# Attention and MLP on one core: native float32 for two units instead of one and a half, the weight decode's word in PSUM, raw weights loaded into their own place

## The chip, the cores and the metric

The kernel runs on one core of a Trainium2 chip. The metric is device microseconds of one execution. The kernel before takes 771.88 us, the median of 3 runs (769.47 to 772.12). The engines are called PE (TensorE), DVE (VectorE), ACT (ScalarE), POOL (GpSimd) and SP (the queue that issues most DMAs).

## The reference

Attention with 4 sink keys and a window of 128, then a two-layer MLP over the 3072 tokens:

```python
# q, k, v: 4 batches, 8 heads, 768 positions, 64 wide; float32
scores = (1 / np.sqrt(64)) * np.matmul(q, k.transpose(0, 1, 3, 2))
keep = is_sink | ((rel >= 0) & (rel < window))        # rel = query position - key position
scores = np.where(keep, scores, -1000000000.0)
scores = scores - np.max(scores, axis=-1, keepdims=True)
a = np.exp(scores)
a = a / (np.sum(a, axis=-1, keepdims=True) + 1e-09)
x = heads_side_by_side(np.matmul(a, v))               # 3072 x 512
h = x @ w_in                                          # 512 x 2048
out = np.maximum(0.01 * h, h) @ w_out                 # 2048 x 512
```

The weights arrive as 64-bit floats and are turned into float32 words on the chip by shifts and masks.

## The kernel before

**Units.** The work is cut into 8 units (`NU`): a batch has two, each with 384 query positions (`TU`), that is `T` = 3 tiles of 128. Tile `s1_3_2` holds the scores of unit 1, head 3, query tile 2. In the first unit of a batch the first query tile sees one block of 128 keys; every other tile sees two blocks, with the 4 sinks between them: 260 columns (`W3`).

**Attention of a head.** `load_head` brings queries and keys, transposed and written twice into 128 rows, `load_next` is called one head ahead. `scores` multiplies; `softmax` on a 260-column tile first writes the previous block's columns over those of the own block that lie in the future (`copy_predicated` with the mask `tri`, the *select*), so that 128 + 4 columns are left, then scales, masks and takes the maximum in one DVE instruction, exponentiates on ACT, and normalises. `tail` transposes on PE, ACT copies the result out of PSUM, and `place` (two affine selects on POOL) separates the two key blocks again. `sinks` gathers the sink columns of a pair of heads, `values` multiplies by v, `emit_x` splits the result into a rounded high part and a rest (`xh`, `xl`).

**Two precisions.** *Native* takes float32 operands as they are, in one product; each is two PE instructions in the profile. *Split* has a high and a low part as `fp32r`, rounded on ACT, the rest by subtraction on POOL or DVE (`split_head`, `split_values`), and two products. `NATH = 9`: the scores of unit 0 and of unit 1's head 0 are native; `NATP = 8`: the values of units 0 and 1 are. All else is split. The MLP is split too, with three products each: `h` in 16 chunks (`fc`) of 12 products, then `o` of 9 products a chunk, which follows one chunk later. `g` is the larger of h and 0.01 h, `gh` and `gl` its parts.

**Weights.** `load_weights(fc)` fetches a raw tile of each matrix (512 KB) into the shared ring `wraw` of two buffers, joins the words on DVE in three steps (L161, L163, L165; the last two read the raw tile and the word, both in SBUF), rounds on ACT (`hi`) and subtracts on POOL (`lo`, L170). `check_weights` later uses the same ring.

**Order.** PE's order is written out by hand: `attention_stream` yields after each tile, and tails, sinks and values stand in the list `pend` until there is credit (`RATE`, `CAP`, `LAG`). Unit 0's attention runs alone, with two chunks decoded meanwhile (`PRE`); then `mlp_stream` takes over and the attention of the next unit is woven in by a due time for each MLP step. Unit 0's MLP also calls `load_weights`, two chunks ahead (`AHEAD`). All other engines' orders come from a scheduler, within the dependences.

**PSUM** has 8 banks: three for o (`ps_o`; during unit 0's attention they hold scores), one each for h (`ps_h`), scores and values, and two for transposes (`ps_t`). Spare matmuls on zeros (`warm`) follow each transpose of unit 0.

Of the kernel before, what the change touches and what calls it, by code (L numbers as in the profile page):

```python
# [117 lines left out]
def fast_path(ctx, tc, cpool, qk, vu, vs, w_in, w_out, out, ident, lim, masks, tri, diag, negm, wmin, wmax):  # L118
# [19 lines left out]

    xs = [[] for _ in range(NU)]
# [5 lines left out]
    def raw_words(nm, fc, name):  # L145
        raw = iopool.tile([P, 512, 2], I32, tag="wraw", name=name, bufs=2)
        if nm == "i":
            src = w_in.rearrange("(c p) f -> p c f", p=P)[:, :, 2 * fc * P:2 * (fc + 1) * P]
            nc.sync.dma_start(out=raw.rearrange("p (c f) t -> p c (f t)", c=NCC), in_=src)
        else:  # L150
            nc.sync.dma_start(out=raw.rearrange("p f t -> p (f t)"), in_=w_out[fc * P:(fc + 1) * P, :])
        return raw

    def load_weights(fc):
        for nm in ("i", "o"):
            raw = raw_words(nm, fc, f"w{nm}raw{fc}")
            top, low = raw[:, :, 1], raw[:, :, 0]
            w = iopool.tile([P, 512], F32, tag="io", name=f"w{nm}{fc}")
            wi = w.bitcast(I32)
            with tc.issue_after(anchor[0].ins):  # L160
                nc.vector.tensor_scalar(out=wi, in0=top, scalar1=3, scalar2=0x3FFFFFFF,  # L161
                                        op0=ALU.logical_shift_left, op1=ALU.bitwise_and)
            nc.vector.scalar_tensor_tensor(out=wi, in0=top, scalar=-0x40000000, in1=wi,  # L163
                                           op0=ALU.bitwise_and, op1=ALU.bitwise_or)
            nc.vector.scalar_tensor_tensor(out=wi, in0=low, scalar=29, in1=wi,  # L165
                                           op0=ALU.logical_shift_right, op1=ALU.bitwise_or)
            hi = wpool.tile([P, 512], F32R, name=f"w{nm}h{fc}")
            lo = wpool.tile([P, 512], F32R, name=f"w{nm}l{fc}")
# [4 lines left out]
    def check_weights(nm, fc):  # L173
        raw = raw_words(nm, fc, f"c{nm}raw{fc}")
# [10 lines left out]
    def native_scores(u, h):  # L185
        return u * H + h < NATH

    def native_values(u, h):
        return NATP0 <= (u * H + h) // 2 < NATP

    def load_head(u, h):
        b, half = divmod(u, 2)
        if native_scores(u, h):
            rows = slice(0, P)
            raw = apool.tile([P, TU + NK[half]], F32, tag="qksp", name=f"qkn{u}_{h}")
        else:
            rows = slice(0, P)
            raw = apool.tile([P, TU + NK[half]], F32, tag="qkraw", name=f"qkraw{u}_{h}", bufs=1)
        nc.sync.dma_start(out=raw[rows, :], in_=qk[half][b, h, rows])
        raws[u, h] = raw  # L200
        if h % 2 == 0:
            if native_values(u, h):
                if h % 4:
                    vr = apool.tile([P, 4 * P], F32, tag="vsp", name=f"vn{u}_{h}", bufs=1)
                else:
                    vr = iopool.tile([P, 4 * P], F32, tag="vraw", name=f"vn{u}_{h}", bufs=1)
                eng = nc.scalar if u + h else nc.sync
            else:
# [40 lines left out]
    wz = wpool.tile([P, TU], mybir.dt.bfloat16, name="wz")  # L249
    nc.gpsimd.memset(wz, 0.0)  # L250

    def keep_warm(u, n):
        if u == 0:
            for _ in range(n):
                nc.tensor.matmul(warm[:, 0:TU], lhsT=wz[:, 0:P], rhs=wz, start=True, stop=True)

    def scores(u, h, j, parts, rows, sp):
# [6 lines left out]
        for c, off in enumerate(parts):  # L264
            nc.tensor.matmul(ps[:, 0:kn], lhsT=sp[rows, off + j * P:off + (j + 1) * P],  # L265
                             rhs=sp[rows, TU + k0:TU + k0 + kn], start=c == 0, stop=c == len(parts) - 1)
        keep_warm(u, WARM)
        return ps

    def softmax(u, h, j, ps, w):  # L270
# [3 lines left out]
        else:  # L274
# [6 lines left out]
                                                   scale=-SCALE * (0.5 if native_scores(u, h) else 1.0), scalar=3.0e38, op0=ALU.add, op1=ALU.min,  # L281
# [19 lines left out]
    slots = [0]  # L301

    def slot():
        slots[0] += 1
        return ps_t.tile([P, P], F32, tag="t", name=f"t{slots[0]}")

    def tail(u, h, j, pk, pt, sk):
# [13 lines left out]
        nc.scalar.copy(out=hi, in_=tp[:, 0:P])
# [396 lines left out]
```

## Time and profile before

| what | value |
|---|---|
| median of 3 runs | 771.88 us (769.47 to 772.12) |
| the profiled execution | 770.29 us, its span 768.5 us |
| mean granted PE clock | 0.984 |
| PE busy | 730.7 us, 95% of the span |
| DVE busy | 586.5 us, 76% |
| ACT busy | 415.3 us, 54% |
| POOL busy | 408.1 us, 53% |
| DMA | 76.73 MB, 100 GB/s in the mean |

Busy time of PE counts a matmul from its start to its modelled end, and matmuls overlap; so two starts in a row tell what one costs in a stream, and the busy share only where PE stands still. Times are counted from the span's start. The span covers 768.5 us of the execution's 770.29.

### The profile page before, as it was taken

How to read it: one execution, taken by the hardware profiler on the slowest of the kernel's cores; microseconds unless marked ns; L12 is line 12 of the kernel's file. 1: busy time of each engine (PE TensorE's matmuls, PEld its weight loads, DVE VectorE, ACT ScalarE, POOL GpSimd, SP SyncE). 2: the span in 40 equal slices, each digit the busy share in tenths (PEclk: the TensorE clock that was granted, in tenths of full speed). 3: DMA queues.
4: the chain of work that ended last, by engine and by line, in shares of the span. 5: the costliest groups of instructions: out<-in, count | busy, mean ns of one | idle time of the engine just before them, and what ended most of it. 6: DMA issues, size and time to landing. Idle time of an engine off the chain costs nothing.

```text
span 768.5 us, 12615 instructions
## 1 busy us (share of the span) xinstructions
PE 730.7 (95%) x3849; PEld 623.9 (81%) x3849; DVE 586.5 (76%) x1884; ACT 415.3 (54%) x1185; POOL 408.1 (53%) x557
## 2 busy tenths in 40 slices
PE   5887898899999999999999999999999999999996
PEld 3445667668888988888888888888898888889895
DVE  7679998997666888888888888888888977733322
ACT  3356555557666566656656566666656555432221
POOL 4237777865455576755665586755665555200000
PEclk8899999999999999999999999999999999999998
DMA  6435555553111243233423442233431321001001
GB/s 237 133 95 174 176 163 169 155 168 123 54 39 63 96 142 101 91 110 115 132 88 96 133 142 95 88 108 123 125 94 63 106 65 40 1 1 42 1 1 46
DMA packets 41707, 76.73 MB, mean 100 GB/s; under 512 B 3616, under 2 KB 24352, under 8 KB 41632
## 3 DMA queue, kind: packets, MB, share of 16 engines
q1 hardware_dynamic: 39920, 73.84, 30.3%
q10 hardware_dynamic: 1712, 2.00, 0.9%
q8 instruction: 33, 0.54, 0.3%
q14 instruction: 42, 0.34, 0.1%
HBM read 69.54 MB, written 6.29 MB: 99 GB/s over the span
## 4 chain that ended last, share of the span: by engine, by line
PE 82%; DVE 11%; DMA 3%; issue 1%; POOL 1%; ACT 0%; DVEq 0%; POOLq 0%; ACTq 0%
PE o L484 33%; PE h L463 32%; PE v L376 9%; PE s L265 5%; PE t L310 2%; DMA woraw<-in_w_out 2%; DVE wo L163 1%; DVE wi L163 1%; DVE wo L161 1%; DVE wi L165 1%; DVE pk L289 1%; DVE pk L280 1%; DVE s L272 1%; DVE wo L165 1%; DVE wi L161 1%
## 5 line engine op out<-in xcount | busy, mean ns | idle before, releaser
L298 POOL TENSOR_SCALAR_AFFINE_SELECT pt<-stg 128x256 fp32r<-128x256 f32 (+1 forms) x320 | 135.5, 448 | 117.8 <-DVE stg L323 50.5
L463 PE MATMUL h<-xh,wih 128*128 128x384 f32 x512 | 189.1, 369 | 5.7 <-DVE g L471 4.6
L463 PE MATMUL h<-xh,wil 128*128 128x384 f32 x512 | 173.6, 339 | 0.8 <-POOL wil L170 0.8
L463 PE MATMUL h<-xl,wih 128*128 128x384 f32 x512 | 173.5, 339 | 0.8 <-DVE xl L426 0.8
L484 PE MATMUL o<-woh,gh 128*128 128x512 f32 x384 | 160.2, 417 | 0.0
L484 PE MATMUL o<-woh,gl 128*128 128x512 f32 x384 | 152.3, 397 | 0.6 <-DVE gl L473 0.5
L484 PE MATMUL o<-wol,gh 128*128 128x512 f32 x384 | 151.6, 395 | 0.0
L471 DVE TENSOR_TENSOR g<-h,g 128x384 f32<-128x384 f32 x128 | 71.0, 554 | 63.7 <-ACT g L470 62.0
L473 DVE TENSOR_TENSOR gl<-g,gh 128x384 fp32r<-128x384 f32 x128 | 103.9, 812 | 17.2 <-ACT gh L472 15.6
L283 ACT ACTIVATE pk<-pk,negm 128x132 f32<-128x132 f32 (+1 forms) x192 | 77.3, 403 | 73.4 <-DVE negm L280 66.4
L463 PEld LDWEIGHTS h<-xh,wih 128*128 128x128 f32 x512 | 96.8, 189 | 23.4 <-DVE g L471 6.0
L226 POOL TENSOR_TENSOR qksp<-qkraw,qksp 64x524 fp32r<-64x524 f32 (+1 forms) x55 | 68.3, 1242 | 74.4 <-issue 54.1
L470 ACT ACTIVATE g<-h 128x384 f32<-128x384 f32 x128 | 62.3, 487 | 72.6 <-PE h L463 72.3
L463 PEld LDWEIGHTS h<-xl,wih 128*128 128x128 f32 x512 | 97.3, 190 | 4.2 <-DVE xl L426 1.1
L463 PEld LDWEIGHTS h<-xh,wil 128*128 128x128 f32 x512 | 96.5, 189 | 1.4 <-POOL wil L170 1.4
L484 PEld LDWEIGHTS o<-woh,gh 128*128 128x128 f32 x384 | 72.4, 188 | 19.1 <-issue 5.5
L484 PEld LDWEIGHTS o<-woh,gl 128*128 128x128 f32 x384 | 72.5, 189 | 18.9 <-DVE gl L473 2.1
L472 ACT CAST gh<-g 128x384 fp32r<-128x384 f32 x128 | 65.7, 513 | 36.3 <-DVE g L471 33.6
L484 PEld LDWEIGHTS o<-wol,gh 128*128 128x128 f32 x384 | 72.7, 189 | 6.4
L265 PEld LDWEIGHTS s<-qksp 128*128 128x128 f32 x330 | 60.7, 189 | 16.8 <-issue 10.2
L265 PE MATMUL s<-qksp 128*128 128x260 f32 (+1 forms) x330 | 65.3, 279 | 8.2 <-DVE negm L280 5.1
L228 POOL TENSOR_TENSOR qksp<-qkraw,qksp 128x384 fp32r<-128x384 f32 x55 | 63.1, 1148 | 4.2
(112 smaller groups left out, 1230.9 us busy)
## 6 DMA issues: line engine op xcount, KB each, us to landing
qkraw<-in_qk SPq DMA_DIRECT2D x31, 454.0 KB, 3.3
qkraw<-in_qk SPq DMA_DIRECT2D x24, 388.0 KB, 3.1
wiraw<-in_w_in SPq DMA_DIRECT2D x16, 512.0 KB, 3.7
woraw<-in_w_out SPq DMA_DIRECT2D x16, 512.0 KB, 3.9
ciraw<-in_w_in SPq DMA_DIRECT2D x16, 512.0 KB, 3.6
coraw<-in_w_out SPq DMA_DIRECT2D x16, 512.0 KB, 3.6
out<-ob SPq DMA_DIRECT2D x23, 256.0 KB, 2.0
qkn<-in_qk SPq DMA_DIRECT2D x8, 388.0 KB, 3.8
```

What stands on the lines that cost most here:

```text
L226: nc.gpsimd.tensor_tensor(out=sp[D:P, TU:TU + n], in0=raw[D:P, TU:TU + n], in1=sp[D:P, TU:TU + n].bitcast(F32), op=ALU.subtract)
L228: nc.gpsimd.tensor_tensor(out=sp[:, TU + n:2 * TU + n], in0=raw[:, 0:TU], in1=sp[:, 0:TU].bitcast(F32), op=ALU.subtract)
L265: nc.tensor.matmul(ps[:, 0:kn], lhsT=sp[rows, off + j * P:off + (j + 1) * P], rhs=sp[rows, TU + k0:TU + k0 + kn], start=c == 0, stop=c == ...
L283: nc.scalar.activation(out=w, in_=w, func=AF.Exp, scale=-1.0, bias=neg, accum_out=sm)
L298: nc.gpsimd.affine_select(out=out, in_=src, pattern=([[0, x]] if x > 1 else []) + [[sign, P]], base=-1 if prev else 0, channel_multiplier= ...
L376: nc.tensor.matmul(out[:, o:o + m], lhsT=l, rhs=r, start=c == 0, stop=c == len(mms) - 1, skip_group_check=True)
L463: nc.tensor.matmul(ph[:, 0:TU], lhsT=w[:, cs], rhs=x, start=cc == 0 and c == 0, stop=cc == NCC - 1 and c == 2)
L470: nc.scalar.mul(g, ph[:, 0:TU], 0.01)
L471: anchor[0] = nc.vector.tensor_tensor(out=g, in0=ph[:, 0:TU], in1=g, op=ALU.max)
L472: nc.scalar.copy(out=gh, in_=g)
L473: (nc.gpsimd if u == 0 and fc % 4 < GLP else nc.vector).tensor_tensor(out=gl, in0=g, in1=gh.bitcast(F32), op=ALU.subtract)
L484: nc.tensor.matmul(po[t], lhsT=gg[:, tsl], rhs=w, start=f == 0 and c == 0, stop=f == NFC - 1 and c == 2)
```

## The change

1. Units 0 and 1 (`EARLY = 2`) are native throughout, scores and values. Their heads go through `attend_early`: three score tiles, `softmax_early` over all 260 columns under a wide mask (made by POOL at the start from the narrow ones), sums of the three tiles in one `[128, 3]` tile, one addition and one reciprocal for the head, then the three normalisations (`normalise_early`, on DVE for unit 0, on ACT for unit 1). No select. `tail_early` transposes both key blocks into one PSUM tile (two transposes), and ACT copies 256 columns to where `values` reads them. No affine select. The sink columns are copied by POOL.
2. `pend` is served by head in units 0 and 1: the tails of a head run beside the next head's scores.
3. Each raw weight tile is loaded into the 4 KB that later hold its `hi` and `lo` (same tag), so no ring is shared; a load waits for the decode of the fourth tile before it (`DEPTH = 4`). The word between the decode steps is an int32 tile in PSUM (tag `d`); the last step writes float32 to SBUF. `ps_t` has one bank for transposes (`t`) and one for the word (`d`); unit 0's attention alternates `t` with `ps_h`, and `d` joins `t` again when all weights are decoded.
4. Three chunks are decoded before the MLP (`PRE = 3`, `PRED = 6`). `gl` of unit 0 moves from DVE to POOL.
5. The sink values are padded from 64 to 128 rows.
6. The spare matmuls after the transposes go; 16 are placed once, behind the first scores.

```diff
-    def raw_words(nm, fc, name):
-        raw = iopool.tile([P, 512, 2], I32, tag="wraw", name=name, bufs=2)
+    decoded = []
     def load_weights(fc):
         for nm in ("i", "o"):
-            raw = raw_words(nm, fc, f"w{nm}raw{fc}")
+            raw = wpool.tile([P, 512, 2], I32, tag=f"w{nm}{fc}", name=f"w{nm}raw{fc}")
+            dma = fetch(raw, nm, fc)
+            if len(decoded) >= DEPTH:
+                tc.add_manual_dep(dma.ins, decoded[-DEPTH].ins.name,
...
+                                  reason="pace")
             top, low = raw[:, :, 1], raw[:, :, 0]
-            w = iopool.tile([P, 512], F32, tag="io", name=f"w{nm}{fc}")
-            wi = w.bitcast(I32)
+            word = ps_t.tile([P, 512], I32, tag="d", name=f"d{nm}{fc}")
+            w = iopool.tile([P, 512], F32, tag="io", name=f"w{nm}f{fc}")
...
-            nc.vector.scalar_tensor_tensor(out=wi, in0=low, scalar=29, in1=wi,
-                                           op0=ALU.logical_shift_right, op1=ALU.bitwise_or)
+            decoded.append(nc.vector.scalar_tensor_tensor(out=w.bitcast(I32), in0=low, scalar=29, in1=word,
+                                                          op0=ALU.logical_shift_right, op1=ALU.bitwise_or))
+            both = wpool.tile([P, 2, 512], F32R, tag=f"w{nm}{fc}", name=f"w{nm}{fc}")
...
+    def softmax_early(u, h, j, ps, w, sm):
+        half = u % 2
+        if half or j:
+            src, mask = ps[:, 0:W3], wide[0 if u == 0 and j == 1 else 1]
+        else:
+            src, w, mask = ps[:, 0:P], w[:, WM:], masks[0]
...
+        anchor[0] = nc.vector.tensor_tensor_reduce(out=w, in0=src, in1=mask, scale=scale(u), scalar=3.0e38,
+                                                   op0=ALU.add, op1=ALU.min, accum_out=neg)
+        nc.scalar.activation(out=w, in_=w, func=AF.Exp, scale=-1.0, bias=neg, accum_out=sm[:, j:j + 1])
+
+    def slot():
+        slots[0] += 1
+        n = slots[0]
+        if phase[0] == 0 and n % 2:
+            return ps_h.tile([P, 512], F32, tag="h", name=f"t{n}")
+        return ps_t.tile([P, 512], F32, tag="d" if phase[0] == 2 and n % 2 else "t", name=f"t{n}")
+
+    def tail_early(u, h, j, w, pt, sk):
+        half = u % 2
+        tp = slot()
+        at = (P if half else 0) + (2 * j - 1) * P
+        if half or j:
+            nc.tensor.transpose(out=tp[:, 0:P], in_=w[:, j, 0:P], identity=ident)
+            nc.tensor.transpose(out=tp[:, P:2 * P], in_=w[:, j, WM:], identity=ident)
+            nc.scalar.copy(out=pt[:, 0, at:at + 2 * P], in_=tp[:, 0:2 * P])
...
-                (nc.gpsimd if u == 0 and fc % 4 < GLP else nc.vector).tensor_tensor(out=gl, in0=g, in1=gh.bitcast(F32), op=ALU.subtract)
+                (nc.gpsimd if u == 0 else nc.vector).tensor_tensor(out=gl, in0=g, in1=gh.bitcast(F32), op=ALU.subtract)
...
+    for _ in range(WARM):
+        nc.tensor.matmul(warm[:, 0:TU], lhsT=wz[:, 0:P], rhs=wz, start=True, stop=True)
```

Three places of the order show what moves. Names are unit, head and tile where the program gives them (`s1_3_2`), or the chunk (`wo6`), followed by a buffer number.

DVE in unit 0's MLP, before, at chunk 4: the decode of chunk 6's second tile, with the select, the tiny sums, and `gl` around it.

```order
L471 TENSOR_TENSOR g0_4_1103<-h0_4_1071,g0_4_1103 128x384
L161 TENSOR_SCALAR wo6_1063<-woraw6_1061 128x512
L272 COPY_PREDICATED s1_3_2_1125<-tri_87,s1_3_2_1125 128x128
L284 TENSOR_SCALAR sm1_3_1_1094<-sm1_3_1_1094 128x1
L163 SCALAR_TENSOR_TENSOR wo6_1063<-woraw6_1061,wo6_1063 128x512
L280 ISA pk1_3_1039,negm_63<-s1_3_2_1125,m2_86 128x132
L280 ISA negm_63 128x1
L285 RECIPROCAL sm1_3_1_1094<-sm1_3_1_1094 128x1
L165 SCALAR_TENSOR_TENSOR wo6_1063<-woraw6_1061,wo6_1063 128x512
L161 TENSOR_SCALAR wi7_1144<-wiraw7_1142 128x512
L272 COPY_PREDICATED s1_4_0_1178<-tri_87,s1_4_0_1178 128x128
L473 TENSOR_TENSOR gl0_4_1105<-g0_4_1103,gh0_4_1104 128x384
```

DVE in unit 0's MLP now, up to chunk 5: `di7` and `do7` are the words in PSUM, `wif7` and `wof7` the decoded tiles.

```order
L170 TENSOR_SCALAR di7_983<-wiraw7_981 128x512
L281 TENSOR_SCALAR sm1_3_866<-sm1_3_866 128x3
L172 SCALAR_TENSOR_TENSOR di7_983<-wiraw7_981,di7_983 128x512
L282 RECIPROCAL sm1_3_866<-sm1_3_866 128x3
L276 ISA pe1_4_1015,negm_63<-s1_4_0_1018,wide1_151 128x260
L276 ISA negm_63 128x1
L174 SCALAR_TENSOR_TENSOR wif7_984<-wiraw7_981,di7_983 128x512
L170 TENSOR_SCALAR do7_993<-woraw7_991 128x512
L276 ISA pe1_4_1015,negm_63<-s1_4_1_1035,wide1_151 128x260
L276 ISA negm_63 128x1
L172 SCALAR_TENSOR_TENSOR do7_993<-woraw7_991,do7_993 128x512
L527 TENSOR_TENSOR g0_5_1028<-h0_5_1001,g0_5_1028 128x384
```

The select and `gl` are gone from DVE, the sums stand once a head, and the decode keeps its distance of two chunks.

PE between chunks 4 and 5 of unit 0's MLP now: `t37` and `t38` are the two remaining transpose groups of unit 1's head 2.

```order
L540 MATMUL o0_2_730<-wo3_696,gh0_3_876 128x512 x2
L540 MATMUL o0_2_730<-wo3_696,gl0_3_877 128x512
L336 MATMUL t37_972<-ident_58,pe1_2_744 128x128
L337 MATMUL t37_972<-ident_58,pe1_2_744 128x128
L336 MATMUL t38_976<-ident_58,pe1_2_744 128x128
L337 MATMUL t38_976<-ident_58,pe1_2_744 128x128
L519 MATMUL h0_5_1001<-xh0_0_352,wi5_836 128x384
```

Each group has two transposes where there was one, and here two groups, which use the same bank, stand with nothing between them.

SP at the start, before: two raw weight tiles (`wiraw0`, `woraw0`) stand ahead of head 2's load, and one head of unit 1 (`qkraw1_1`) too.

```order
L199 DMA qkn0_1_153<-in_qk0 128x776
L149 DMA wiraw0_221<-in_w_in 128x4x256
L151 DMA woraw0_231<-in_w_out 128x1024
L199 DMA qkraw1_1_629<-in_qk1 128x908
L199 DMA qkn0_2_183<-in_qk0 128x776
L199 DMA qkn0_3_249<-in_qk0 128x776
```

SP at the start now; `ciraw0` is the first tile that `check_weights` will read.

```order
L202 DMA qkn0_1_184<-in_qk0 128x776
L202 DMA qkraw0_2_187<-in_qk0 128x776
L153 DMA wiraw0_247<-in_w_in 128x4x256
L154 DMA woraw0_257<-in_w_out 128x1024
L153 DMA wiraw1_306<-in_w_in 128x4x256
L154 DMA woraw1_316<-in_w_out 128x1024
L153 DMA ciraw0_3055<-in_w_in 128x4x256
L202 DMA qkn0_3_213<-in_qk0 128x776
```

Head 2's load has moved ahead of the weights, head 3's behind five raw tiles.

More of the change, by code (lines that the diff above doesn't have):

```diff
@@ L137, in fast_path @@
         sts.append(st)
+    wide = []
+    for n, m in enumerate(masks[1:]):
+        e = apool.tile([P, W3], F32, tag="stg", name=f"wide{n}")
+        for sign, base, dst in ((1, -1, e[:, 0:P]), (-1, 0, e[:, WM:])):
+            nc.gpsimd.affine_select(out=dst, in_=m[:, NSK:], pattern=[[sign, P]], base=base,
+                                    channel_multiplier=-sign, compare_op=ALU.is_ge, fill=-MASKED)
+        nc.gpsimd.tensor_copy(out=e[:, P:WM], in_=m[:, 0:NSK])
+        wide.append(e)
     xs = [[] for _ in range(NU)]
@@ L247, in fast_path, with scale, scores @@
     warm = ps_h.tile([P, 512], F32, tag="h", name="warm")
[L249 to L257, printed above, removed]
+    def scale(u):
+        return -SCALE / 2 if u < EARLY else -SCALE
+    def scores(u, h, j, parts, sp):
         k0, kn = KSL[u % 2][j]
@@ L301, in fast_path @@
     slots = [0]
+    phase = [0]
     def slot():
         slots[0] += 1
-        return ps_t.tile([P, P], F32, tag="t", name=f"t{slots[0]}")
+        n = slots[0]
[10 more added lines that the diff above has]
+            nc.scalar.copy(out=pt[:, 0, at:at + 2 * P], in_=tp[:, 0:2 * P])
+        else:
+            nc.tensor.transpose(out=tp[:, 0:P], in_=w[:, j, WM:], identity=ident)
+            nc.scalar.copy(out=pt[:, 0, 0:P], in_=tp[:, 0:P])
+        if j == T - 1:
+            nj = T - 1 + half
+            nc.gpsimd.tensor_copy(out=sk[:, 0:nj, h % 2], in_=w[:, T - nj:, P:WM])
     def tail(u, h, j, pk, pt, sk):
@@ L406, in attend @@
         sk = state["sk"]
[L407 removed]
+        pt = apool.tile([P, 2, 2 * TU], F32R, tag="pt", name=f"pt{u}_{h}")
         state["pt", odd] = pt
         for j in range(T):
[L410 removed]
+            ps = scores(u, h, j, (0, TU + NK[u % 2]), sp)
             softmax(u, h, j, ps, pk[:, j, :])
@@ L425, in emit_x @@
         nc.scalar.copy(out=xh, in_=x)
-        (nc.gpsimd if u < XLP and not native_values(u, 2 * pair) else nc.vector).tensor_tensor(out=xl, in0=x, in1=xh.bitcast(F32), op=ALU.subtract)
+        (nc.gpsimd if EARLY <= u < XLP else nc.vector).tensor_tensor(out=xl, in0=x, in1=xh.bitcast(F32), op=ALU.subtract)
         xs[u].append((xh, xl))
```

199 lines of the change are left out of this document (108 added, 91 removed).

## The prediction

> **What bounds the kernel now.** I read the profile's page first, then the busy times by stage, then the chain of waits in the stage that is not full, then single instructions there.
>
> ```profile
> PE 730.7 (95%) x3849; PEld 623.9 (81%) x3849; DVE 586.5 (76%) x1884; ACT 415.3 (54%) x1185; POOL 408.1 (53%) x557
> PEclk8899999999999999999999999999999999999998
> ```
>
> PE is the fullest engine, but an average hides stages. The next view cuts the span at four moments: 5.91 is the first matmul, 34.82 the first score of unit 0's head 5, 57.24 the first MLP matmul, 170.49 the start of chunk 15 (the last) of unit 0's MLP. Columns: length, then busy time and count of PE, PEld, DVE, ACT, POOL, then granted clock, DMA share, GB/s.
>
> ```profile
> 5.91:34.82 28.91, 23.08 (x80) 13.81 (x80) 24.31 (x116) 11.88 (x47) 11.56 (x21) 0.76 0.63 211
> 34.82:57.24 22.42, 19.90 (x95) 11.15 (x94) 15.56 (x82) 10.64 (x43) 7.30 (x20) 1.00 0.27 84
> 57.24:170.49 113.25, 97.22 (x463) 73.34 (x463) 106.85 (x248) 62.67 (x169) 85.39 (x91) 0.97 0.55 170
> 170.49:768.50 598.01, 590.53 (x3215) 525.63 (x3213) 437.51 (x1430) 328.80 (x926) 301.59 (x415) 1.00 0.26 81
> ```
>
> After 170.49 PE is full until the last stores, and the change leaves that work alone. From 57.24 to 170.49, where unit 0's MLP runs, unit 1's attention beside it and the weights are decoded, DVE is busy 106.85 of 113.25 us and PE waits. The chain of waits confirms it (start, length, what):
>
> ```profile
> 88.73 3.99 DMA woraw<-in_w_out
> 94.25 1.48 DVE wo L163
> 113.62 4.29 DMA woraw<-in_w_out
> 138.95 3.98 DMA woraw<-in_w_out
> 151.33 4.01 DMA wiraw<-in_w_in
> 156.44 1.70 DVE wi L163
> ```
>
> The chain runs from decode step to decode step, and four times through a whole raw-weight load, 16.3 us together: with two raw buffers a load can start only when an older raw tile has been read. Single instructions of this stage, from the timeline:
>
> ```profile
> 102.06 0.42 DVE L161 TENSOR_SCALAR wo<-woraw 128x512 int32<-128x512 int32 x1
> 102.60 1.58 DVE L163 SCALAR_TENSOR_TENSOR wo<-woraw,wo 128x512 int32<-128x512 int32 x1
> 102.14 1.49 POOL L170 TENSOR_TENSOR wil<-wi,wih 128x512 fp32r<-128x512 f32 x1 [0.41 <-ACT wih L169]
> 112.17 0.69 DVE L163 SCALAR_TENSOR_TENSOR wo<-woraw,wo 128x512 int32<-128x512 int32 x1
> ```
>
> The same L163 takes 1.58 us while POOL subtracts and 0.69 while POOL is idle.
>
> **The stage 57.24 to 170.49, DVE's side.** Its groups there (busy, mean ns):
>
> ```profile
> L163 DVE SCALAR_TENSOR_TENSOR wi<-wiraw,wi 128x512 int32<-128x512 int32 x14 | 15.3, 1096 | 0.1
> L163 DVE SCALAR_TENSOR_TENSOR wo<-woraw,wo 128x512 int32<-128x512 int32 x14 | 15.1, 1081 | 0.1
> L165 DVE SCALAR_TENSOR_TENSOR wi<-wiraw,wi 128x512 int32<-128x512 int32 x14 | 14.6, 1040 | 0.1
> L165 DVE SCALAR_TENSOR_TENSOR wo<-woraw,wo 128x512 int32<-128x512 int32 x13 | 11.9, 919 | 0.0
> L473 DVE TENSOR_TENSOR gl<-g,gh 128x384 fp32r<-128x384 f32 x15 | 9.4, 629 | 0.0
> L272 DVE COPY_PREDICATED s<-tri,s 128x128 f32<-128x128 int8 x22 | 6.3, 284 | 1.7 <-PE s L265 1.7
> L333 DVE COPY sk<-pk 128x12 f32<-128x12 f32 x7 | 4.0, 565 | 0.2 <-ACT pk L287 0.2
> ```
>
> - Removed from DVE: the selects (6.3 us, fewer than three of 22 remain), the sink copies of unit 1 (4.0), gl of unit 0 (9.4, now on POOL). About 19.
> - The word in PSUM: 55 two-input decode steps average (15.3+15.1+14.6+11.9)/55 = 1.03 us. Each now reads one operand from SBUF and one from PSUM. Bounds: 0.69, the undisturbed row, to 1.03, if the excess stays. I take 0.69, because the disturbed rows are those with POOL reading SBUF beside them: minus 19 us.
> - The first decode step now writes PSUM; no row shows that. Bounds 0.42 (undisturbed, to SBUF) and 0.69 (the same 512 columns at a two-input step's pace). I take 0.69; with 26 steps at most plus 7 us.
> - The 260-column softmax: the step from 128 columns (0.284) to 512 (0.69) is 1.06 ns a column, so 128 columns more cost 0.14 us, 19 times: plus 2.6. The sum's two tiny operations run once a head, not thrice: a gain I leave uncounted.
>
> Sum: 106.85 - 19 - 19 + 7 + 2.6 = 78 us. With PE at 94 (below), DVE is no longer the slower engine. If the excess stays in the two-input steps, it is 97.
>
> [...]
>
> POOL has 85.39 us in the stage. It loses unit 1's two selects a tile (L298) and seven heads' splitting, and gains 15 gl at about 1 us. I cost this at nothing: a gl queues behind one decode subtraction (1.49) at most, and its reader, the second MLP product, stands a whole chunk later on PE.
>
> **PE's side.** Start-to-start times from the full stretch, and the native forms from where they run undisturbed:
>
> ```profile
> 57.24 0.44 PE L463 MATMUL h<-xh,wih 128*128 128x384 f32 x1
> ...
> 170.49 0.34 PE L463 MATMUL h<-xh,wih 128*128 128x384 f32 x1
> ...
> 171.02 0.40 PE L265 MATMUL s<-qksp 128*128 128x260 f32 x2
> 171.26 0.34 PE L463 MATMUL h<-xh,wih 128*128 128x384 f32 x1
> ...
> 172.31 0.27 PE L310 MATMUL t<-ident,pk 128*128 128x128 f32 x1
> 172.34 0.42 PE L463 MATMUL h<-xh,wih 128*128 128x384 f32 x1
> 172.60 0.34 PE L463 MATMUL h<-xl,wih 128*128 128x384 f32 x1
> ...
> 172.95 0.39 PE L484 MATMUL o<-woh,gh 128*128 128x512 f32 x1
> ...
> 173.64 0.40 PE L265 MATMUL s<-qksp 128*128 128x260 f32 x2
> ```
>
> ```profile
> 39.80 0.60 PE L265 MATMUL s<-qkn 128*128 128x260 f32 x2
> 40.25 0.30 PE L310 MATMUL t<-ident,pk 128*128 128x128 f32 x1
> ...
> 79.39 1.51 PE L376 MATMUL v<-pt,vn 128*64 128x128 f32 x8
> 80.83 0.85 PE L376 MATMUL v<-sn,vsraw 24*64 24x384 f32 x2
> 81.62 0.44 PE L463 MATMUL h<-xh,wih 128*128 128x384 f32 x1
> ```
>
> From them: an h step (171.02-170.49)/3 = 0.177, an o step (173.64-172.95)/3 = 0.23, a split score tile 171.26-171.02 = 0.24, a native one 40.25-39.80 = 0.45 (0.49 allowed, since others stand behind values), a transpose 0.29-0.177 = 0.11, one head's values 81.62-79.39 = 2.23.
>
> The orders give the counts between the first h and chunk 15. Both: 180 h (31.7 us), 126 o (29.0), 8 heads of values (17.8), 4 sink transposes (0.4). Before, also 22 wide and 2 narrow split tiles (5.5) and 24 transposes (2.6): 87.0 us of work in 113.25. After, 19 native tiles (9.3), 4 split ones (0.7), 49 transposes (5.4): 94.3. So the change adds 7.3 us of PE work and uncovers up to 26 us of waiting.
>
> What is late next? Two things. The ph bank is single, and DVE's max on it still stands behind a decode step: about 0.2 us in each of 15 chunks, 3 us. And until the last weight is decoded the transposes have one PSUM bank, where they had two. Three groups stand within 0.65 us of the one ahead (the order shows one pair back to back); the next are 1.05 to 1.3 us apart.
>
> ```profile
> 128.28 0.27 PE L310 MATMUL t<-ident,pk 128*128 128x128 f32 x1
> 128.87 0.26 ACT L321 COPY stg<-t 128x128 f32<-128x128 f32 x1
> ```
>
> From a transpose's start to the end of its copy 0.85 us pass here. Three close groups and some of the others make 3 us; I add 2 for the clock and the start. 94.3 + 8 = 102 us for the stage, 11 less than before.
>
> **From 5.91 to 57.24.** DVE carries six decoded tiles instead of four, some 2 us each undisturbed (0.69 x 3), so plus 4; against that, two selects, two thirds of the tiny operations and the sink copy of each head, and no split or POOL select between the transpose's copy and the values. PE loses 24 spare matmuls, gains 16 transposes (1.8) and two score tiles of unit 1 (1.0). The 16 spare ones stand behind head 0's scores, while head 0's softmax runs and PE has nothing else. The wide masks are made on POOL ahead of head 0's second tile, which waits for them; POOL is otherwise idle then. The queue of SP carries four raw tiles and one check tile ahead of head 3's load; at 211 GB/s five tiles of 0.52 MB are 12 us, and heads 1 and 2 are there to work on: no loss. Bounds: 6.9 us gained (28.91 x 0.24, if the clock stays up) to 4 us lost (the two decoded tiles). I take a gain of 3 by the missing POOL step; the granted 0.76 has no cause that the change surely removes.
>
> **Sum.** 11 + 3 = 14 us off the profiled execution's 770.29 us (span 768.5, 1.8 around it) gives 756.3. The median of the three runs is 771.88, 1.6 above that execution; I say **757**. The padded sinks (32 KB more a load, never waited for) cost nothing: DMA has a share of 0.26 in the long stage.
>
> **Rivals.**
> - *The transposes' single bank decides (slower).* 28 groups use it. ACT is in order: the profile shows a copy at 0.85 us, but if decode casts and 260-column exponentials stand ahead of it, every group waits. It decides from a wait of 19/28 = 0.7 us a group, which eats the whole gain beside the 94.3. At 1.2 us a group the stage is 94.3 + 5 + 34 = 133: 770.3 + 20 - 3 = 787. Against it: ACT is busy 62.67 of 113.25. Chance 0.07.
> - *Decode stays the pace.* The two-input steps stay at 1.03 us in PSUM, or the raw loads, which now wait for the fourth decode before and stand on SP behind head loads that wait for PE, are late as before. DVE then has 97 us and its in-order waits; the stage takes 109 to 113 and the time is 764 to 770. For it: four loads on the chain; against it, four tiles ahead instead of two. Chance 0.2.
> - *Everything fits and the clock stays up.* Stage 97, start 6 us shorter: 770.3 - 16 - 6 = 748. Chance 0.13. [...]
> - *My forecast*, 752 to 763: 0.57. Something else: 0.03.
>
> **How the numbers follow.** A change under 0.5% (3.9 us) could hardly be told from none. Faster: forecast 0.57, the full case 0.13 and two thirds of the decode case, 0.84; same: the rest of that case and a remainder, 0.08; slower 0.08. Range 747 (the full case and 1 us) to 768 (most of the decode case); likeliest alone 752 to 763.
>
> **What would show it.** Right: decode steps at 0.69 us with little spread, none of the raw loads on the chain, first h near 54, chunk 15 near 156, PE full from about 65, the tail from chunk 15 again 598 us. Wrong: DVE over 90 us between those moments; PE waiting for copies out of t; raw loads still on the chain; or a first h past 58, if the extra decoding sits on head 1's path.

## The result, and the profile after

| | before | after |
|---|---|---|
| median | 770.67 us (769.11 to 772.12, 4 runs) | 748.86 us (746.63 to 749.65, 4 runs) |
| profiled execution, its span | 770.29, 768.5 us | 746.63, 745.1 us |
| mean granted PE clock | 0.984 | 0.992 |

The ratio of after to before is 0.9713, 95% interval 0.9679 to 0.9746. The time lies inside the range of 747 to 768 us, 8 us below the 757 given as likeliest, and below that one's own range of 752 to 763.

The profiled execution is the fastest of the four; the other three took 1.5 to 3 us more. The page of the kernel after, busy time of the engines and the granted clock in 40 slices:

```profile
PE 714.3 (96%) x3881; PEld 620.6 (83%) x3881; DVE 549.3 (74%) x1749; ACT 420.6 (56%) x1178; POOL 370.0 (50%) x500
PEclk9899999999999999999999999999999999999999
```

The busy times by stage, cut as in the prediction (6.12 the first matmul, 33.27 the first score of head 5, 58.74 the first MLP matmul, 161.57 the start of chunk 15; columns: length, then busy time and count of PE, PEld, DVE, ACT, POOL, clock, DMA share, GB/s):

```profile
6.12:33.27 27.15, 19.42 (x84) 12.50 (x85) 24.83 (x81) 13.76 (x46) 8.71 (x15) 0.87 0.86 291
33.27:58.74 25.47, 22.70 (x100) 12.59 (x99) 12.80 (x57) 12.92 (x47) 2.22 (x6) 0.94 0.45 133
58.74:161.57 102.83, 97.35 (x486) 76.22 (x486) 76.55 (x174) 64.06 (x164) 56.42 (x56) 1.00 0.54 160
161.57:745.10 583.53, 574.84 (x3215) 519.32 (x3213) 432.70 (x1427) 328.55 (x921) 300.31 (x414) 1.00 0.27 84
```

Against the rows of before:

| stretch | before | forecast | after |
|---|---|---|---|
| up to the first MLP matmul | 57.24 | about 54 | 58.74 |
| from there to chunk 15 (the *stage*) | 113.25 | 102 | 102.83 |
| from chunk 15 to the end (the *tail*) | 598.0 | 598 | 583.5 |

The stage came as forecast. The start came 1.5 us later where 3 us sooner was forecast, and 14.5 of the 23.4 us that the span lost came from the tail, where nothing was forecast. The tail has the same 3215 PE instructions in both. So three questions: what the tail gained, what carried the stage, why the start gained nothing.

### The profile page after: what moved, and what is told of

It reads as the page before. It is cut to its first block, busy times and chain, and to the rows that moved or that the text cites. A ratio compares the mean times of both kernels' runs of the same rounds, so it can differ in the third digit from the quotient of the medians.

```text
span 745.1 us, 12489 instructions
## 1 busy us (share of the span) xinstructions
PE 714.3 (96%) x3881; PEld 620.6 (83%) x3881; DVE 549.3 (74%) x1749; ACT 420.6 (56%) x1178; POOL 370.0 (50%) x500
## 4 chain that ended last, share of the span: by engine, by line
PE 84%; DVE 9%; ACT 3%; issue 1%; DMA 1%; ACTq 0%; SPq 0%; DVEq 0%
PE o L540 32%; PE h L519 31%; PE v L406 10%; PE s L264 7%; PE t L349 2%; DVE gl L529 2%; DVE zeroi L192 1%; PE t L336 1%; DMA qkn<-in_qk 1%; DVE g L527 1%; DVE pe L276 0%; DVE xf L415 0%; DVE pk L309 0%; PE t L370 0%; PE t L337 0%
## 5 line engine op out<-in xcount | busy, mean ns | idle before, releaser
L519 PE MATMUL h<-xh,wi 128*128 128x384 f32 x1024 | 314.9, 354 | 1.6 <-DVE g L527 1.6
L540 PE MATMUL o<-wo,gh 128*128 128x512 f32 x768 | 244.4, 399 | 0.0
L519 PEld LDWEIGHTS h<-xh,wi 128*128 128x128 f32 x1024 | 190.0, 188 | 16.6 <-issue 2.9
L519 PE MATMUL h<-xl,wi 128*128 128x384 f32 x512 | 172.5, 337 | 0.0
L540 PE MATMUL o<-wo,gl 128*128 128x512 f32 x384 | 151.5, 394 | 0.0
L540 PEld LDWEIGHTS o<-wo,gh 128*128 128x128 f32 x768 | 133.7, 188 | 18.2 <-issue 2.4
L318 POOL TENSOR_SCALAR_AFFINE_SELECT pt<-stg 128x256 fp32r<-128x256 f32 x240 | 101.3, 447 | 83.4 <-DVE stg L357 70.1
L519 PEld LDWEIGHTS h<-xl,wi 128*128 128x128 f32 x512 | 96.9, 189 | 3.6 <-DVE xl L475 0.2
L230 POOL TENSOR_TENSOR qksp<-qkraw,qksp 64x392 fp32r<-64x392 f32 (+1 forms) x48 | 58.4, 1218 | 64.2 <-issue 47.5
L540 PEld LDWEIGHTS o<-wo,gl 128*128 128x128 f32 x384 | 72.2, 188 | 16.7 <-DVE gl L529 0.3
```

Source lines behind the costliest of these rows:

```text
L230: nc.gpsimd.tensor_tensor(out=sp[D:P, TU:TU + n], in0=raw[D:P, TU:TU + n], in1=sp[D:P, TU:TU + n].bitcast(F32), op=ALU.subtract)
L318: nc.gpsimd.affine_select(out=out, in_=src, pattern=([[0, x]] if x > 1 else []) + [[sign, P]], base=-1 if prev else 0, channel_multiplier= ...
L519: nc.tensor.matmul(ph[:, 0:TU], lhsT=w[:, cs], rhs=x, start=cc == 0 and c == 0, stop=cc == NCC - 1 and c == 2)
L540: nc.tensor.matmul(po[t], lhsT=gg[:, tsl], rhs=w, start=f == 0 and c == 0, stop=f == NFC - 1 and c == 2)
```

## The tail: 64 rows or 128

Full stretches of two whole units (chunk 0 of unit 4 to chunk 0 of unit 6), before and after, one row of the windows each:

```profile
433.08:605.49 172.41, 172.41 (x954) 153.47 (x953) 146.69 (x487) 106.01 (x304) 109.61 (x145) 1.00 0.34 105
```

```profile
417.40:585.84 168.44, 167.88 (x954) 151.49 (x953) 145.85 (x487) 106.40 (x304) 109.92 (x145) 1.00 0.36 112
```

PE is busy without a gap in the first, with the same 954 instructions, at full clock, and takes 4.0 us more. One place differs, the sinks' product at the end of each head's values. PE's timeline of before, then of after:

```profile
441.71 1.03 PE L376 MATMUL v<-pt,vsp 128*128 128x128 f32 x8
442.67 0.44 PE L376 MATMUL v<-st,ssp 64*128 64x384 f32 x1
443.04 0.50 PE L484 MATMUL o<-woh,gh 128*128 128x512 f32 x1
443.37 0.39 PE L484 MATMUL o<-wol,gh 128*128 128x512 f32 x1
```

```profile
426.00 1.04 PE L406 MATMUL v<-pt,vsp 128*128 128x128 f32 x8
426.87 0.39 PE L406 MATMUL v<-st,ssp 128*128 128x384 f32 x1
427.10 0.63 PE L540 MATMUL o<-wo,gh 128*128 128x512 f32 x2
```

Read the starts. Ahead of the 64-row product the eight matmuls take 0.96 us, ahead of the 128-row one 0.87. The product takes 0.37 and 0.23. The `o` behind the 64-row product takes 0.33, where a usual one takes 0.23. So PE loses about 0.1 us on going in, 0.13 in it and 0.1 on coming out, although the product has half as many rows (64*128 against 128*128). Added up by the starts, the sixteen products of two units lose 5.1 us. Of these 4.0 are left in the whole, 0.25 for each product. PE, now ahead, waits 0.56 us of the rest (without work in the second row); the last half microsecond was not traced. All 48 such products of units 2 to 7 stand in the tail.

*The kernel before with padded sinks alone:*

```diff
-SKR = 64
+SKR = P
-    vs = np.zeros((B, NPAIR, 2, SKL, 2, D), v.dtype)
+    vs = np.zeros((B, NPAIR, SKR // SKL, SKL, 2, D), v.dtype)
-            vs[:, :, :, r + x * NSK:r + (x + 1) * NSK, x] = s4[:, :, None, x]
+            vs[:, :, 0:2, r + x * NSK:r + (x + 1) * NSK, x] = s4[:, :, None, x]
```

> The kernel before with one edit: the sinks' operands have 128 rows instead of 64, the 72 that hold nothing set to zero. Theory A: a matmul over 64 rows costs PE extra each time it stands among matmuls over 128 rows. In the trace of before two units with 16 such matmuls take 4.0 us longer than in the trace after, 0.25 us for each, and about 50 of them stand behind chunk 15. Then the stretch from chunk 15 to the end falls from 598 to about 584 us and the time from 770.5 to 756 or 757, with nothing else changed. Rival B: the gain in that stretch comes from something else in the change (hi and lo of a weight in one tile, fewer selects on DVE, POOL's lighter load), and the padding is free as predicted. Then the stretch stays 598 and the time 770 to 771.

Measured: 761.13 us (761.01 to 761.72), ratio to the kernel before 0.9881 (0.9861 to 0.9901). Its stages, and the two units:

```profile
57.46:174.90 117.44, 99.38 (x464) 76.09 (x463) 108.97 (x249) 63.35 (x171) 86.53 (x92) 0.94 0.54 167
174.90:759.30 584.40, 576.30 (x3215) 520.07 (x3213) 434.50 (x1429) 329.42 (x924) 301.29 (x414) 1.00 0.28 84
431.06:599.57 168.51, 168.03 (x954) 151.56 (x953) 146.01 (x487) 106.45 (x304) 110.16 (x145) 1.00 0.36 109
```

The tail fell from 598.0 to 584.4 and the two units from 172.41 to 168.51. The whole gained 10 us rather than 14, since the stage, which this edit hardly touches, lost 4 at a clock of 0.94. PE waits 12.0 us there for DVE's maxima (L280), 5.1 before; why is open.

*The changed kernel with 64 rows again:*

```diff
-SKR = P
+SKR = 64
```

> The changed kernel with the sinks' operands over 64 rows again. Theory A (64 rows cost PE 0.25 us each): the stretch from chunk 15 to the end rises from 583.5 to about 598 us, the time from 749 to 762 or 763. Rival B (padding is free): 749 and 583.5.

Measured: 762.28 us (761.73 to 763.12), ratio 0.9893 (0.9872 to 0.9914). The tail, and the two units:

```profile
165.07:760.80 595.73, 589.06 (x3215) 524.76 (x3213) 435.15 (x1427) 327.23 (x921) 299.65 (x414) 1.00 0.26 81
427.68:600.17 172.49, 172.49 (x955) 153.53 (x955) 147.21 (x487) 105.93 (x304) 109.76 (x145) 1.00 0.35 108
```

Done alone or undone alone, the row count moves the tail by 13.6 and 12.2 us. Theory A holds; 48 x 0.25 is 12 us. At the same row count the rest of the change is worth 1 to 2 us in the tail (598.0 to 595.7, 584.4 to 583.5), which is not settled. The 64-row product among 128-row ones pays on both sides, by the starts 0.1 us ahead of it and 0.1 behind; by what mechanism is not shown by any run.

*The same for the first two units*, whose native sinks' products have 16 or 24 rows and write 64 columns:

```diff
-        sn = xpool.tile([SROWS, T, P], F32, tag="xf", ...)
+        sn = xpool.tile([P if u < EARLY else SROWS, T, P], F32, tag="xf", ...)
+        if u < EARLY:
+            nc.gpsimd.memset(sn[:, 0:nj, :], 0.0)
...
-            return sv
+            return sn[:, 0:nj, :].rearrange("p j q -> p (j q)")
```

> The changed kernel with the sinks' products of the first two units over 128 rows as well (a zeroed 128-row tile instead of 16 or 24 rows; one POOL memset a pair is added). Theory A: what the padding does in the later units it does here: 16 products, two matmuls each, now 0.57 (256 columns) and 0.79 us (384 columns) with a change of rows before and after, fall to about 0.4 and 0.55 and let the next instruction start 0.1 us sooner: 3 to 5 us in all, half of it in the stage from the first MLP matmul to chunk 15 (about 100.5 instead of 102.8), time 744 to 746. Rival B: these products write 64 columns of the array and change its form anyway, so padding saves nothing there: 747 to 750.

Measured: 747.10 us (745.80 to 748.83), ratio 0.9693 (0.9676 to 0.9710), which overlaps the changed kernel's; the stage took 103.3 us, the tail 583.4. By its starts a 384-column product takes 0.74 us instead of 0.79, a 256-column one 0.53 instead of 0.57, and the matmuls ahead of each take 0.09 us less (1.35 instead of 1.44, 1.13 instead of 1.22): 0.14 us for each of 16, some 2 us in all. The `h` behind takes 0.28 us with and without padding, where a usual one takes 0.17. So neither theory: half of what A expected, and too little to stand out in the time. That the 64 columns are what is left to pay was not tried.

## The stage: the word in PSUM

DVE's groups in the stage after (mean ns behind the busy time):

```profile
L172 DVE SCALAR_TENSOR_TENSOR di<-wiraw,di 128x512 int32<-128x512 int32 x13 | 9.0, 693 | 0.3
L170 DVE TENSOR_SCALAR do<-woraw 128x512 int32<-128x512 int32 x13 | 9.0, 692 | 0.3
L174 DVE SCALAR_TENSOR_TENSOR wof<-woraw,do 128x512 int32<-128x512 int32 x13 | 8.8, 680 | 0.5
```

Every decode step takes 0.68 to 0.69 us in the mean; for the two-input steps (L172, L174) that is the undisturbed value (0.67 to 0.69 us in the kernel before, where nothing runs on POOL). It makes no difference here whether POOL subtracts meanwhile: none of those beside a subtraction takes more than 0.71 us. Two that overlap:

```profile
88.74 0.69 DVE L172 SCALAR_TENSOR_TENSOR do<-woraw,do 128x512 int32<-128x512 int32 x1
88.81 1.30 POOL L179 TENSOR_TENSOR wi<-wif,wi 128x512 fp32r<-128x512 f32 x1 [5.68 <-PE s L264]
```

What PE waits for in the stage after (us in total, times, longest):

```profile
PE t L336 <- DVE wof L174: 2.0, 1, 2.0
PE t L336 <- ACT pt L338: 1.9, 4, 0.7
PE h L519 <- DVE g L527: 1.6, 1, 1.6
```

Three experiments take the decode apart. *The word back in SBUF:*

```diff
-            word = ps_t.tile([P, 512], I32, tag="d", name=f"d{nm}{fc}")
             w = iopool.tile([P, 512], F32, tag="io", name=f"w{nm}f{fc}")
+            word = w.bitcast(I32)
```

> The changed kernel with the decode's intermediate word in SBUF (in the decoded tile itself) instead of PSUM. Theory A: the word in PSUM is what brought the two-input decode steps from 1.03 to 0.69 us. They go back to about 1.0 us, the first step to 0.42, so DVE has 52 x 0.34 less 26 x 0.27 more, 11 us, in the stage from the first MLP matmul to chunk 15: 76.5 to 87. PE has 97 us there, so only in-order waits show: stage 104 to 110 instead of 102.8, time 750 to 756. Rival B: the steps were slow for another reason (two raw tiles and two decoded ones in flight beside the splitting on POOL that unit 1 no longer has), and stay 0.69 or less in SBUF too: stage 99 to 103, time 747 to 749.

Measured: 760.43 us (759.43 to 761.74), ratio 0.9867 (0.9844 to 0.9890). The stage, and DVE's groups in it:

```profile
65.41:176.57 111.16, 98.35 (x486) 75.94 (x486) 87.32 (x174) 63.14 (x164) 65.63 (x56) 1.00 0.46 148
```

```profile
L172 DVE SCALAR_TENSOR_TENSOR wif<-wiraw,wif 128x512 int32<-128x512 int32 x13 | 13.3, 1021 | 0.2
L174 DVE SCALAR_TENSOR_TENSOR wof<-woraw,wof 128x512 int32<-128x512 int32 x13 | 11.5, 883 | 0.1
```

A two-input step beside a subtraction in this kernel:

```profile
75.97 1.67 POOL L179 TENSOR_TENSOR wo<-wof,wo 128x512 fp32r<-128x512 f32 x1 [0.95 <-ACT wo L178]
76.53 1.66 DVE L174 SCALAR_TENSOR_TENSOR wif<-wiraw,wif 128x512 int32<-128x512 int32 x1
```

Where nothing runs on POOL, the two-input steps take 0.65 to 0.69 us here too (twenty of them). So here, with both inputs in SBUF, a step and the subtraction beside it took 1.66 and 1.67 us, and with one input in PSUM 0.69 and 1.30 (a subtraction of the changed kernel with no decode step beside it takes 1.27 to 1.31).

DVE's sum is the expected 87 us, yet the stage took 111, and the first MLP matmul came at 65.41. DVE is not full; what PE waits for longest in the stage is ACT's copies out of the transposes' bank, 4.9 us where the changed kernel has 1.9. ACT has the casts of the decoded tiles in its order, and it waits 19.8 us for those tiles, 8.7 in the changed kernel. Theory A, undersized by the waits behind the longer steps.

*The kernel before with the word in PSUM.* It has no free bank, so the word takes one of the two for transposes, throughout:

```diff
-    ps_t = ctx.enter_context(tc.tile_pool(name="ps_t", bufs=2, space=PSUM))
+    ps_t = ctx.enter_context(tc.tile_pool(name="ps_t", bufs=1, space=PSUM))
...
-            wi = w.bitcast(I32)
+            wi = ps_t.tile([P, 512], I32, tag="d", name=f"d{nm}{fc}")
```

> The kernel before with the decode's word in a PSUM bank of its own, which takes the second bank of the transposes; nothing else changed. Theory A (the prediction's): the two-input decode steps fall from 1.03 to 0.69 us for the most part, DVE's 106.85 us in the stage from the first MLP matmul to chunk 15 fall to about 95, but the raw loads still wait for one of two raw tiles and the selects stay on DVE: stage 105 to 110 instead of 113.25, time 764 to 768. Rival B: the word in PSUM gives nothing alone, since the loads and the single bank of the transposes set the pace: 770 to 774.

Measured: 796.78 us (794.75 to 797.18), ratio 1.0313 (1.0279 to 1.0347), outside both expectations. The stages:

```profile
5.90:68.23 62.33, 51.35 (x174) 28.42 (x174) 42.81 (x197) 24.21 (x91) 19.98 (x43) 0.73 0.42 134
68.23:170.21 101.98, 93.05 (x464) 70.95 (x463) 88.34 (x249) 62.71 (x169) 66.66 (x90) 1.00 0.61 186
170.21:794.80 624.59, 596.91 (x3215) 523.52 (x3213) 440.33 (x1429) 334.05 (x925) 302.48 (x415) 1.00 0.25 78
```

The stage falls from 113.25 to 101.98 us, as much as the whole change brought there, and theory A was too timid about it. POOL gains as well: its 46 selects (L298) take 0.31 us in the mean instead of 0.54. Not all of it need be the word: the start is 11 us longer here, so a load of unit 1's keys (`qkraw`) is issued 2 us ahead of the first MLP matmul, where the kernel before issues it 5 us behind and has it for 4.68 us on its chain of waits (the prediction's list leaves it out). What that is worth was not tried. What loses is the bank: 11 us at the start and 27 in the tail. PE's waits in that tail, of which the kernel before has none:

```profile
PE t L310 <- DVE sm L284: 8.1, 8, 1.0
PE t L310 <- DVE pt L323: 7.5, 10, 0.9
PE t L310 <- DVE stg L323: 3.3, 6, 0.9
```

That is the prediction's slower rival, seen at work. The change escapes it by `slot`: before the MLP the transposes share the bank of h, and from the last decode on they have the word's bank again. This run changes two things at once; that the bank, and not the word, costs the 38 us rests on these waits, which are 18.9 of the 27 us in the tail. At the start PE's transposes wait 8.2 us for ACT's copies (L321), and the clock is 0.73 instead of 0.87.

*Two raw tiles in flight instead of four, in the changed kernel:*

```diff
-DEPTH = 4
+DEPTH = 2
```

> The changed kernel with a raw load that waits for the second decode before instead of the fourth: as with two raw buffers before, only two raw tiles are in flight. Theory A: fetching in place with four in flight took the four waits for raw loads (16.3 us) off the chain, but with DVE at 76.5 of 102.8 us most of that cover is now spare: stage from the first MLP matmul to chunk 15 is 103 to 107, time 749 to 753. Rival B: the depth carries the stage's gain: loads return to the chain four times at 4 us, stage 110 to 117, time 757 to 764.

Measured: 755.14 us (754.14 to 756.35), ratio 0.9799 (0.9777 to 0.9822). DVE's groups in the stage, with their idle time and what ended it:

```profile
L170 DVE TENSOR_SCALAR di<-wiraw 128x512 int32<-128x512 int32 x13 | 9.0, 694 | 3.1 <-DMA wiraw<-in_w_in 3.0
L170 DVE TENSOR_SCALAR do<-woraw 128x512 int32<-128x512 int32 x13 | 9.0, 693 | 7.0 <-DMA woraw<-in_w_out 6.9
```

Five raw loads are back on the chain of waits, 21 us together, the first and the last of them:

```profile
94.00 4.35 DMA woraw<-in_w_out
...
148.63 5.36 DMA woraw<-in_w_out
```

The stage takes 108.84 us, between the two expectations: four raw tiles in flight instead of two are worth 6 us to it. The kernel before with the word in PSUM also has two raw tiles only, and 102 us; but PE has 93.05 us of work there, the changed kernel 97.35.

## The start: six experiments

PE's timeline of the changed kernel around the two longest waits (idle time and releaser in brackets):

```profile
16.91 0.45 PE L340 MATMUL t<-ident,pe 128*128 128x128 f32 x1 [3.06 <-DVE pe L288]
20.70 2.21 PE L406 MATMUL v<-pt,vraw 128*64 128x256 f32 x6
31.79 0.30 PE L340 MATMUL t<-ident,pe 128*128 128x128 f32 x1 [3.16 <-DVE pe L288]
33.84 2.40 PE L406 MATMUL v<-pt,vn 128*64 128x256 f32 x6
37.40 1.30 PE L406 MATMUL v<-pt,vn 128*64 128x256 f32 x6
```

PE waits for the division (L288) of heads 1 and 3, and then six matmuls take 2.21 and 2.40 us, at a granted clock of 0.56 and 0.50, that take 1.30 at a clock of 1.00 (37.40). DVE ahead of the first of these divisions:

```profile
14.43 0.69 DVE L172 SCALAR_TENSOR_TENSOR di<-wiraw,di 128x512 int32<-128x512 int32 x1
15.03 0.16 DVE L281 TENSOR_SCALAR sm<-sm 128x3 f32<-128x3 f32 x1
15.16 0.69 DVE L174 SCALAR_TENSOR_TENSOR wif<-wiraw,di 128x512 int32<-128x512 int32 x1
15.76 0.17 DVE L282 RECIPROCAL sm<-sm 128x3 f32<-128x3 f32 x1
15.88 0.69 DVE L170 TENSOR_SCALAR do<-woraw 128x512 int32<-128x512 int32 x1
16.48 1.81 DVE L288 TENSOR_SCALAR pe<-pe,sm 128x128 f32<-128x128 f32 x3
```

Three decode steps, 2.1 us, stand between the head's last exponential on ACT (its sum is there at 14.2) and its division. Since sums and reciprocal are taken once for all three tiles, the first tile's division waits for the last tile too. Each experiment changes one thing of the changed kernel, the last one two:

| edit | time, us | ratio to before | first MLP matmul | stage |
|---|---|---|---|---|
| none | 748.86 | 0.9713 (0.9679 to 0.9746) | 58.74 | 102.83 |
| decode at steps 17, 33, 49 (`PRE0 = 2`, `PRED = 16`) | 752.33 | 0.9761 (0.9744 to 0.9778) | 64.80 | 101.92 |
| 14 spare matmuls in each of the two waits | 748.26 | 0.9712 (0.9695 to 0.9729) | 60.60 | 101.89 |
| no spare matmuls (`WARM = 0`) | 746.33 | 0.9692 (0.9671 to 0.9713) | 58.78 | 101.94 |
| unit 0's division on ACT | 750.82 | 0.9730 (0.9703 to 0.9756) | 63.26 | 101.92 |
| two chunks ahead (`PRE = 2`) | 745.04 | 0.9647 (0.9622 to 0.9672) | 58.36 | 101.57 |
| `PRE = 2` and `WARM = 0` | 742.01 | 0.9626 (0.9601 to 0.9651) | 55.90 | 103.10 |

The last two columns are of the profiled execution. The tail is 583.5 to 584.1 us in all seven. A single first MLP matmul says little: the changed kernel with 64 rows, whose work up to there is the same, has it at 62.16, with a clock of 0.85 up to there instead of 0.90.

> The changed kernel with the three chunks that are decoded ahead of the MLP placed at attention steps 17, 33 and 49 instead of 9, 15 and 21: on DVE they then stand beside the softmax of heads 3, 5 and 7, when PE has values to compute, and no longer between head 1's softmax and its division. Theory A: the first MLP matmul came 1.5 us later than before because the decode steps stand in front of the division of heads 1 and 3 (PE waits 3.06 and 3.16 us there, and its clock falls behind each). Then these waits go, PE's clock stays up through the values, the first MLP matmul comes at 51 to 54 us instead of 58.7, and the time is 742 to 745. Rival B: the waits come from the chain of a head itself (softmax, exponential, sum, division), and decode only fills them: first MLP matmul 57 to 59, time 747 to 750.

```diff
-PRE0 = 4
+PRE0 = 2
-PRED = 6
+PRED = 16
```

Slower, and neither theory. The first wait shrank from 3.06 to 1.27 us, and the first pair's values came 2.65 us sooner, as A says. But the moved steps now meet later maxima (L276). PE's timeline of this kernel:

```profile
40.33 0.33 PE L336 MATMUL t<-ident,pe 128*128 128x128 f32 x1 [1.23 <-DVE negm L276]
...
54.01 0.70 PE L264 MATMUL s<-qkraw 128*128 128x260 f32 x2 [2.43 <-DVE negm L276]
```

The granted clock is 0.77 from 36 to 46 us and 0.84 from 46 to 56, where the changed kernel has 0.99 and 1.00.

> The changed kernel with 14 spare matmuls (0.176 us each, 2.5 us) ahead of the first transpose of heads 1 and 3 of unit 0, where PE waits 3.06 and 3.16 us and the granted clock then falls to half in the trace after. Theory A: the waits themselves stay, but what follows them is no longer at half clock, so the values of the first two pairs take 1.3 us a half pair instead of up to 2.4, and the first MLP matmul comes at 53 to 56 us instead of 58.7; time 743 to 746, with less spread from run to run. Rival B: the half clock has another cause than these two waits; then the start and the time stay within 1.5 us of the changed kernel's (747 to 750).

```diff
+        for _ in range(14 if u == 0 and j == 0 and h in (1, 3) else 0):
+            nc.tensor.matmul(tp[:, 0:TU], lhsT=wz[:, 0:P], rhs=wz, start=True, stop=True)
```

The clock did stay up through the first pair of heads, 1.00 instead of 0.67 from 16 to 26 us: with matmuls in the two waits it does not fall there; and the time did not move. The windows from 16 to 26 us, of the changed kernel and of this one:

```profile
16.00:26.00 10.00, 8.27 (x29) 4.88 (x30) 9.85 (x24) 3.64 (x10) 4.26 (x5) 0.67 0.77 251
```

```profile
16.00:26.00 10.00, 8.27 (x42) 4.75 (x41) 9.03 (x27) 4.04 (x14) 2.95 (x4) 1.00 0.67 206
```

DVE is busy 9.85 and 9.03 of the 10 us. What the clock gives back is waited away at a later division: PE waits 2.45 us for that of head 5, 0.35 in the changed kernel. Rival B in the time, but not by its reason.

> The changed kernel without its 16 spare matmuls behind head 0's scores. Theory A (the clock is lost in the later waits for DVE, whatever stood before): within 2 us of the changed kernel, 747 to 751, first MLP matmul 57 to 61. Rival B (the spare matmuls hold the clock through head 0's softmax and all that follows): the granted clock falls from 9 us on, the first MLP matmul comes 2 to 4 us later, the time is 751 to 754.

```diff
-WARM = 16
+WARM = 0
```

The 16 spare matmuls do nothing for the clock that the time shows (746.33 us without them, 748.86 with): theory A, 0.7 us below its range, and if anything a gain, but the intervals of the two overlap.

> The changed kernel with unit 0's division of the softmax by its sums (24 instructions, 8.6 us on DVE before the first MLP matmul) on ACT, as unit 1 has it. Theory A: PE waits three times, 6.6 us, for exactly this division, behind decode steps on DVE; on ACT nothing of the decode stands ahead of it but casts of 0.62 us, so at least half of the waits goes: first MLP matmul 54 to 56 us, time 743 to 746. Rival B: ACT's own exponentials (0.48 us and a 0.19 us read of the sum each) make the chain as long: first MLP matmul 58 to 60, time 747 to 751.

```diff
-            if u:
+            if True:
                 nc.scalar.mul(p, p, sm[:, j:j + 1])
```

Rival B in the time, with a first MLP matmul 3 us later than even B had it: the same three waits, 6.0 us, now end on ACT.

> The changed kernel with two chunks decoded ahead of the MLP instead of three; the third is decoded behind the first MLP matmul. Theory A: the two decoded tiles more, some 2 us each on DVE, are why the first MLP matmul is late: without them it comes 2 to 4 us sooner (55 to 57 us), and the stage behind it, where DVE is busy 76.5 of 102.8, takes up the 4 us for 1 at most; time 745 to 747. Rival B: they only fill gaps of DVE's in heads 3 and 4, and the waits belong to the chain of a head: first MLP matmul 58 to 60, time 748 to 751, since the third chunk now stands in front of the stage's own work.

```diff
-PRE = 3
+PRE = 2
```

Theory A in the time: faster than the changed kernel, with intervals that do not overlap. PE's wait at head 3 fell from 3.16 to 1.69 us, that at head 1, which stands behind the first chunk, stayed at 3.05. The profiled first MLP matmul moved by 0.4 us only: this execution was already 0.9 us later at head 1 (17.80 instead of 16.91). The stage takes up the chunk's decoding without loss.

> The changed kernel with two chunks decoded ahead of the MLP instead of three, and without the 16 spare matmuls: the two edits that came out ahead of it, together. Theory A: they save different things (4 us of DVE's work before the first MLP matmul, and 2.8 us of PE's behind head 0's scores), so the gains of 3.8 and 2.5 us add up: 741.5 to 743.5, with the stage from the first MLP matmul at 101 to 102 us and the first MLP matmul at 55.5 to 57. Rival B: both act on the same waits for DVE in heads 1 and 3 and on the clock behind them, and are not additive: 744 to 747, first MLP matmul 58 to 59.

`PRE = 2` and `WARM = 0` together. 742.01 us (741.76 to 744.69), theory A, with a stage of 103.1 us where it had 101 to 102: the two gains, 3.8 and 2.5 us, add up by their medians, though the second is not clear of the noise. It is the fastest of all, ahead of the changed kernel by about 7 us.

So what helped was to take DVE work out of the start, into the stage, where DVE has room; spreading it within the start, handing the division to ACT or keeping the clock up did not. How much of each start is the clock's stays open, since only one execution of each kernel is profiled.

## Why the prediction was right, and where not

- **The stage, 102 against 102.83: right, by its mechanism.** 78 us of DVE was forecast, 76.55 measured; decode steps at 0.69, the 260-column softmax at 0.42. Back in SBUF the word costs 8 us in the stage; put into PSUM in the kernel before, it goes with a stage of 102 us. The granted clock in the stage was 1.00 where it had been 0.97. That a step with one input in PSUM would run at the undisturbed 0.69 beside POOL was the author's estimate, which no run showed when it was made; now the steps beside a subtraction are measured at 0.67 to 0.71 us. Inside PE's side two terms were off and cancelled: its work is 97.4 us instead of 94.3, its waits 5.5 instead of 8.
- **One row was misread.** At 112.17 POOL was not idle: it ran two selects, and the second, which lay beside the 0.69 us step, took 0.77 us instead of the 0.31 of the run with the word in PSUM. There it was POOL that took longer. The value 0.69 holds all the same, by the steps with POOL idle, 0.67 to 0.69 us.

```profile
112.25 0.77 POOL L298 TENSOR_SCALAR_AFFINE_SELECT pt<-stg 128x128 f32<-128x128 f32 x1
```

- **"The padded sinks cost nothing": the step that failed most.** It priced the padding by its bytes alone and never asked what 64 rows cost PE. The 0.33 us `o` behind the product stood in the trace of before. It measured 12 to 14 us of gain, so "the change leaves that work alone" was wrong for the tail.
- **The start, 3 us sooner forecast, 1.5 later measured: failed.** It credited the missing POOL step with more than the two extra decoded tiles cost. They are not hidden: they are decoded from 27.0 to 32.8 us, where PE waits 3.16 us for the division of head 3, and without them it waits 1.69. "A first h past 58, if the extra decoding sits on head 1's path" named it.
- **The sum: too large in its own terms.** They were 11 and 3 us and measured 10.4 and -1.5, 8.9 us instead of 14. The change with 64 rows shows what they give: 762.28 us, inside the range, at the upper end of 752 to 763. That the time came out below the forecast and not above it is the padding's doing, which no term held: luck. (756.3 and 1.6 also make 757.9, not 757.)
- **The rivals.** Decode did not stay the pace; the single bank did not decide here, because the change gives it back in time, though it can (the kernel before with one bank: 27 us in the tail). "Everything fits" gave 748, right in the time by luck: its start, 6 us shorter, was wrong, and the tail's gain was not in it.

## What to carry to other kernels

Price a change of shape on the engine that runs it, not by its bytes: where a product with fewer rows stands among full ones, compare the starts just ahead of and behind it, and pad with zeros if they lag (here 0.25 us a product, 12 to 14 us in the tail). An operand moved to PSUM can free a contended DVE (here 76.55 us of work in the stage instead of 87.32), but count the banks, and give the bank back when the phase ends (the kernel before, with one bank for the transposes throughout, took 38 us more in its start and its tail). In a start where engines wait for each other in turn, move work out to a stage with room (3.8 us here) rather than about within the start.

## What the hardware did that was not expected

- A 64-row product of 384 columns takes 0.37 us where one over 128 rows takes 0.23, and costs its neighbours 0.1 us each (0.96 instead of 0.87 ahead, 0.33 instead of 0.23 behind).
- A lower PE clock did not show in the time where PE waits for another engine: with 0.67 and, by spare matmuls, 1.00 between 16 and 26 us, the medians are 748.86 and 748.26.
- The first decode step, with one input, takes 0.69 us into PSUM and, in the kernel before, 0.42 into SBUF with nothing on POOL (0.66 and 0.79 in the mean of its stage, for the two weights), and still the word in PSUM wins: the stage took 102.83 us with it and 111.16 without.
